# The first batch's last nine hidden units computed as sums of parts behind most of its down products

## Chip, cores and metric

The kernel runs on one core of a Trainium2 chip. The metric is device time in microseconds (us), the median of several runs. A page of one profiled execution and its trace go with it. The engines are TensorE (PE, with its weight loads as PEld), VectorE (DVE), ScalarE (ACT), GpSimd (POOL) and SyncE (SP), which issues nearly all the DMAs.

## The reference

Two blocks follow each other. The first is a linear attention on sketches: q and k of shape (4 batches, 4 heads, 1088 tokens, 32) are projected with S1 and S2 to 8 values each, and their outer product gives 64 features.

```python
def phi(x):
    a = np.einsum('rd,bhsd->bhsr', S1, x)
    b = np.einsum('rd,bhsd->bhsr', S2, x)
    return np.einsum('bhsi,bhsj->bhsij', a, b).reshape(*x.shape[:-1], r * r)
q_p, k_p = (phi(q), phi(k))
kv = np.einsum('bhsf,bhsd->bhfd', k_p, v)
z = np.sum(k_p, axis=2)
num = np.einsum('bhsf,bhfd->bhsd', q_p, kv)
den = np.einsum('bhsf,bhf->bhs', q_p, z)[..., None] + 1e-06
return (num / den).astype(np.float32)
```

The result, 4352 tokens of 128 values, is x of the second block, a SwiGLU feed-forward net with 1536 hidden values:

```python
g = x @ w_gate
silu = g * (1.0 / (1.0 + np.exp(-g)))
val = x @ w_val
return (silu * val @ w_out).astype(np.float32)
```

## The kernel before

Tokens lie along the free axis (`xT`, 128 x 4352). They are cut into blocks: 0, 1 and 2 are the first batch (384, 384 and 320 tokens), blocks 3 to 9 the other three batches (six of 480 and one of 384). The 1536 hidden values are 12 chunks of 128. A *unit* (i, j) is block i and chunk j: gate and value products into two PSUM banks, SiLU on ACT, the product of both on VectorE into a slot of `hbuf` or `late`. `down` (L1061) multiplies one such chunk with w_out and adds up 12 of them in one bank; `store` (L1120) transposes the sum on VectorE and writes it out.

A unit is computed in one of two ways. `unit` (L1026) uses two fp32 matmuls, each of which the profile shows as two records. `start_unit` (L990) and `finish_unit` (L1002) use parts: weights and tokens are cut into a high part, a scaled low part and a difference (`w1`, `wb`, `wd`; `x1`, `x0`, `xd`) of type fp32r, and the product is three fp32r matmuls of one record each. `start_unit` does the difference products (L997) and lets ACT scale both banks (L1000); `finish_unit` adds the other two products per bank (L1010, L1011), then ACT's SiLU (L1013) and VectorE's product (L1018). The parts of weights are made by `cut_weights` (L840), three chunks of 128 at a time ("chunk 3" of a weight below is its hidden chunks 9 to 11): ACT makes w1, VectorE (for wg) or POOL (for wv) the low part, ACT wb, and VectorE or POOL the difference. `cut_tokens` (L873) does the same for one block of tokens.

Before, blocks 0 to 2 are all computed with `unit`, and blocks 3 to 9 with the parts. The weights come as 64-bit numbers and are narrowed to fp32 by `narrow` (L245), with rotating buffers `exp` and `man`.

The attention of batches 1 to 3 runs beside this as a generator, `attentions` (L615): `parts_of(n)` lets it go n steps on. Its steps for a batch are transposes of k and q on VectorE, key products on TensorE (L354), key features on VectorE (L377), sums of the key features on POOL (`feature_sums`, L543), key values on TensorE (L388), query sketches (L342) with copies on ACT (L590), denominators and query features on VectorE (`query_step`, L741), and numerators on TensorE (L780).

Every engine works through its own list in the order in which the program writes it; semaphores keep the dependences. So the place of a step in this order decides what it stands behind on each engine. Around the change the order is written out by hand, in the loop over `seq` (L1300): 30 units of the first batch, from the 18th on (z = 17) with one down product and one step of the attention each, and with the pieces of `cut_weights` put between. Six early units keep SiLU and value apart (`late=True`), and `catch_up` (L1055) multiplies them later on POOL. After the loop the remaining down products run three at a time with further steps of the attention (L1345 to 1355), then the first main unit is started (L1358). The main loop (L1376) does 84 units.

PSUM has eight banks. `bank` hands out four single ones, `pair` the least recently used of three pairs that is not held, and `wide` the pairs named "a" and "b".

Of the kernel before, what the change touches and what calls it, by code (L numbers as in the profile page):

```python
# [19 lines left out]
def kernel(  # L20
# [223 lines left out]

    def narrow(dst, raw, shape, engine=nc.gpsimd, split=False):  # L245
# [14 lines left out]
            stage.tile(shape, I32, tag=n + tag, name=n, bufs=6) for n in ("exp", "man")  # L260
# [282 lines left out]
    def feature_sums(phk):  # L543

        rows = phk[:].rearrange("p c h i j -> p c (h i j)")
        s = apool.tile([P, 4, H * F], FP32, tag="zs", name="zs")
        add = lambda o, a, b: nc.gpsimd.tensor_tensor(out=o, in0=a, in1=b, op=ALU.add)

        def last():
            add(s[:, 0, :], s[:, 0, :], s[:, 1, :])  # L550
            add(s[:, 0, :], s[:, 0, :], rows[:, 8, :])

        return s[:, 0, :], [
            lambda: add(s[:, 0:2, :], rows[:, 0:2, :], rows[:, 4:6, :]),
            lambda: add(s[:, 2:4, :], rows[:, 2:4, :], rows[:, 6:8, :]),
            lambda: add(s[:, 0:2, :], s[:, 0:2, :], s[:, 2:4, :]),
            last,
        ]
# [56 lines left out]
    def attentions():  # L615
# [5 lines left out]
        hold("a")  # L621
        kp = wide("a")
# [11 lines left out]
        for n, (i, c0, c1) in enumerate(((0, 0, 3), (0, 3, 5), (1, 5, 7), (1, 7, 9))):  # L634
            first = H * (c0 - kpieces[i][0])
            kb = sketch(kp, i)[:, first : first + H * (c1 - c0), 1, :]
            key_features(phk, (ka[:, H * c0 : H * c1, :], kb), c0, c1)
            if n == 3:
                release("a")
            if n % 3 != 1:  # L640
                yield
        zs, sums = feature_sums(phk)
        for f in sums:
            f()
        yield from turn_keys(2)
        kvz = wide("a")
        key_values(kvz[:, 0, 0:F], phk, 0, NC)
        value_sums(kvz[:, 0, :], zs)
        kab, kcopies = sketched(wide("b"), key_products, 2, "kab2")
        fold(kvz[:, 0, :])  # L650
        spread = spread_out(1, kvz[:, 0, :])
        hold("a", "b")
        yield
        qab, copies = sketched(wide("a"), query_sketches, 3, "qab")
        run_copies(copies, 2)
        yield
        run_copies(kcopies, 2)
        release("a", "b")
# [165 lines left out]
    def homes(w):  # L824


        if w is wv:
            for c in range(4):
                yield [
                    stage.tile([P, 3, P], F32R, tag=tag, name=name, bufs=6)[:]  # L830
                    for tag, name in (("exp", "w1"), ("man", "wb"), (("exp", "man")[c % 2], "wd"))
                ]
        else:
            big = lambda pool, tag, bufs: pool.tile([P, 2, 3, P], F32R, tag=tag, name="g" + tag, bufs=bufs)
            for c in range(2):
                t = [big(stage, "raw", NRAW), big(stage, "raw", NRAW), big(apool, "phq", 2)]
                for k in range(2):
                    yield [x[:, k] for x in t]

    def cut_weights(w, lows, engine):  # L840
# [3 lines left out]
        for c, (w1, wb, wd) in enumerate(homes(w)):  # L844
            src = w[:, 3 * c : 3 * c + 3, :]
            low = lows[c]
            w_parts[id(w), c] = (w1, wb, wd)
            fine = dict(out=wd, in0=whole(w1), in1=whole(wb), **sub), engine.tensor_tensor
            if engine is nc.vector:
                fine = dict(  # L850
                    out=wd, in0=low, scalar=-BETA, in1=whole(w1), op0=ALU.mult, op1=ALU.add
                ), engine.scalar_tensor_tensor
            for row, f, args in zip(
                rows,
                (nc.scalar.activation, engine.tensor_tensor, nc.scalar.activation, fine[1]),
                (
                    dict(out=w1, in_=src, func=AF.Copy, scale=CUT),
                    dict(out=low, in0=src, in1=whole(w1), **sub),
                    dict(out=wb, in_=low, func=AF.Copy, scale=BETA),
                    fine[0],  # L860
                ),
            ):
                row.append((f, args))
# [9 lines left out]
    def cut_tokens(i, engine=nc.gpsimd):  # L873
# [21 lines left out]
        first, second = (difference, low) if engine is nc.vector else (low, difference)  # L895
# [94 lines left out]
    def start_unit(y):  # L990

        i, j = line[y // NCH], y % NCH
        n = blocks[i][1]
        xd = x_parts[i][2][:, 0:n]
        ps = sums_of[y] = pair(y)[:, :, 0:n]
# [6 lines left out]
    def finish_unit(y):  # L1002
        i, j = line[y // NCH], y % NCH
        n = blocks[i][1]
        x1, x0, _ = (x[:, 0:n] for x in x_parts[i])
        ps = sums_of.pop(y)
# [14 lines left out]
        let_go(y)  # L1021
# [39 lines left out]
    def down(y=None):  # L1061
# [3 lines left out]
        if j == 0:  # L1065
            acc[i] = bank("g1" if i == 1 else "g2" if i in line[2::2] else "acc")
# [231 lines left out]
    seq += [(i, j) for j0 in (6, 9) for i in range(3) for j in range(j0, j0 + 3)]  # L1298
    order = [(i, j) for i in range(3) for j in range(NCH)]
    for z, (i, j) in enumerate(seq):  # L1300
# [6 lines left out]
        if z in (24, 25, 26):  # L1307
            catch_up()
# [4 lines left out]
        if z >= 17:  # L1313
            todo.remove(order[0])
            todo.insert(0, order.pop(0))
            down()
        if z == 20:
            lows = [
                pool.tile([P, 3, P], FP32, tag=tag, name="low", bufs=bufs)[:]
                for pool, tag, bufs in ((apool, "qb", 2), (apool, "dT", 2), (apool, "rd", 2), (apool, "qb", 2))  # L1320
            ]
            first, low, second, third = cut_weights(wv, lows, nc.gpsimd)
        if z in (20, 21):
            take(first, 2)
        if z == 21:
            take(low, 3)
        if z == 25:
            take(second, 3)
        if z >= 17:
            parts_of(1)  # L1330
        if z == 26:
            take(low, 1)
            take(third, 3)
        if z == 29:
            take(second, 1)
            take(third, 1)
        if z == 23:
            lows = [room[:, 6 + c, :].rearrange("p (c f) -> p c f", f=P) for c in range(4)]
            gates = cut_weights(wg, lows, nc.vector)
        for row, at in enumerate(((23, 24), (25, 26, 27, 28), (27, 28))):  # L1340
            if z in at:
                take(gates[row], 4 // len(at))
    todo.sort()
    x_steps = None
    while len(todo) > 2:  # L1345
        for _ in range(min(3, len(todo) - 2)):
            down()
        if len(todo) < 9:
            take(gates[3], 2)
        if begun[0] and not x_steps:  # L1350
            x_steps = cut_tokens(HEAD, nc.vector)
            run(x_steps)
        parts_of(1 + (begun[0] and len(todo) > 2))
    while not begun[0]:
        parts_of(1)
    run(x_steps or cut_tokens(HEAD, nc.vector))
    hold("acc")
    start_unit(0)  # L1358
    while todo:
        down()  # L1360
# [15 lines left out]
    for y in range(END):  # L1376
        if y in GROUPS:
            group()
        if y in WIDE:
            finish_unit(y)  # L1380
        if y + 1 < END:
            start_unit(y + 1)
        if y not in WIDE:
            finish_unit(y)
# [52 lines left out]
```

## Time and profile before

| | |
|---|---|
| median of 3 runs | 278.81 us (278.68 to 279.05) |
| profiled execution | 278.89 us, its span 277.2 us |
| TensorE busy | 271.4 us, 98% of the span |
| VectorE busy | 203.7 us, 74% |
| ScalarE busy | 184.5 us, 67% |
| GpSimd busy | 98.9 us, 36% |
| down products (L1082) on the chain that ended last | 22% |
| fp32 units (L1034) on that chain | 16% |
| parts products (L997, L1010, L1011) on that chain | 13% each |
| first parts product of a main unit (L997) in the timeline | 91.42 us |

How to read it: a busy TensorE overlaps itself, since matmuls are pipelined; the pieces of the chain show how long each one holds the next. The idle time of an engine counts only where another one waits for it. A row of the timeline has the start, the duration, the engine, the line, and output and inputs by name.

### The profile page before, as it was taken

What the parts mean: (1) busy time and instruction counts of PE and PEld (TensorE: products, weight loads), DVE (VectorE), ACT (ScalarE), POOL (GpSimd) and SP (SyncE); (2) the same over time, 40 slices, a digit from 0 to 9 for tenths busy, and PEclk for the clock granted to TensorE, in tenths of its full rate; (3) what the DMA queues carried; (4) which work ended last, traced back from release to release, by engine and by line L of the source; (5) the groups of instructions that cost most, each with busy time, mean ns of one, the idle gap of its engine ahead of it and who ended that gap; (6) DMA issues with size and microseconds to landing.
All of it is one profiled execution on the core that took longest, in us unless ns stands there. A gap on an engine that the chain in (4) does not pass through costs nothing.

```text
span 277.2 us, 5670 instructions
## 1 busy us (share of the span) xinstructions
PE 271.4 (98%) x2169; PEld 198.3 (72%) x2169; DVE 203.7 (74%) x355; ACT 184.5 (67%) x330; POOL 98.9 (36%) x110
## 2 busy tenths in 40 slices
PE   8899999999999999999999999999999999999995
PEld 7645565666766787777577777867887888788994
DVE  3997987977688873887545766967877995987431
ACT  3468665565421586667479898769879878886860
POOL 3313422179820440060034353435425553542000
PEclk9999999999999999999999999999999999999999
DMA  6573195221151123000200020000100200010011
GB/s 192 168 220 79 54 277 185 74 89 57 39 114 28 26 85 94 2 1 0 38 13 4 0 39 0 0 2 10 27 0 2 36 0 1 9 29 0 10 29 28
DMA packets 26139, 14.30 MB, mean 52 GB/s; under 512 B 19840, under 2 KB 24192, under 8 KB 26112
## 3 DMA queue, kind: packets, MB, share of 16 engines
q1 hardware_dynamic: 25456, 13.84, 19.4%
q8 instruction: 17, 0.28, 0.4%
q10 hardware_dynamic: 656, 0.10, 0.2%
q14 instruction: 10, 0.08, 0.1%
HBM read 11.41 MB, written 2.23 MB: 49 GB/s over the span
## 4 chain that ended last, share of the span: by engine, by line
PE 94%; DVE 2%; DMA 2%; ACT 1%; issue 0%; SPq 0%
PE PS L1082 22%; PE PS L1034 16%; PE PS L1010 13%; PE PS L997 13%; PE PS L1011 13%; PE PS L1074 2%; PE PS L1077 2%; PE PS L1076 2%; PE PS L354 2%; PE PS L780 2%; PE PS L342 2%; PE PS L388 2%; DMA kld<-in_k_dram 2%; PE PS L1110 1%; PE PS L497 1%; PE PS L445 1%
## 5 line engine op out<-in xcount | busy, mean ns | idle before, releaser
L1000 ACT ACTIVATE PS<-PS 128x960 f32<-128x960 f32 (+1 forms) x84 | 78.5, 935 | 32.0 <-PE PS L997 31.2
L1018 DVE SCALAR_TENSOR_TENSOR hbuf<-PS,sg 128x480 f32<-128x480 f32 (+1 forms) x84 | 53.7, 640 | 43.6 <-ACT sg L1013 40.8
L1013 ACT ACTIVATE sg<-PS 128x480 f32<-128x480 f32 (+1 forms) x84 | 46.7, 556 | 2.0 <-PE PS L1011 1.2
L997 PE MATMUL PS<-xd,gphq 128*128 128x480 f32 (+1 forms) x84 | 47.3, 564 | 0.0
L1082 PE MATMUL PS<-hbuf,wo 128*128 128x480 f32 (+3 forms) x118 | 45.9, 492 | 0.0
L1010 PE MATMUL PS<-x,graw 128*128 128x480 f32 (+1 forms) x84 | 32.1, 382 | 0.0
L1011 PE MATMUL PS<-x,wb 128*128 128x480 f32 (+1 forms) x84 | 31.6, 376 | 0.0
L997 PE MATMUL PS<-xd,wd 128*128 128x480 f32 (+1 forms) x84 | 31.4, 374 | 0.0
L1010 PE MATMUL PS<-x,w 128*128 128x480 f32 (+1 forms) x84 | 31.4, 374 | 0.0
L1011 PE MATMUL PS<-x,graw 128*128 128x480 f32 (+1 forms) x84 | 31.3, 373 | 0.0
L1034 PE MATMUL PS<-xT,wg 128*128 128x384 f32 (+1 forms) x72 | 28.7, 480 | 0.0
L1034 PE MATMUL PS<-xT,wv 128*128 128x384 f32 (+1 forms) x72 | 28.0, 470 | 0.2 <-DVE wv L286 0.2
L1082 PEld LDWEIGHTS PS<-hbuf,wo 128*128 128x128 f32 x118 | 22.1, 189 | 7.4 <-issue 0.9
L1038 ACT ACTIVATE sg<-PS 128x384 f32<-128x384 f32 (+1 forms) x30 | 13.8, 465 | 18.8 <-PE PS L1034 17.2
L997 PEld LDWEIGHTS PS<-xd,gphq 128*128 128x128 f32 x84 | 15.8, 188 | 10.0 <-ACT PS L1000 6.4
L997 PEld LDWEIGHTS PS<-xd,wd 128*128 128x128 f32 x84 | 15.8, 189 | 9.9 <-issue 6.7
L884 POOL TENSOR_TENSOR x<-xT,x 128x480 fp32r<-128x480 f32 (+1 forms) x6 | 7.2, 1195 | 37.6 <-ACT x L881 37.6
L1034 PEld LDWEIGHTS PS<-xT,wv 128*128 128x128 f32 x72 | 13.4, 190 | 8.9 <-DVE hbuf L1049 0.9
L1034 PEld LDWEIGHTS PS<-xT,wg 128*128 128x128 f32 x72 | 12.9, 189 | 9.3 <-issue 1.2
L1010 PEld LDWEIGHTS PS<-x,graw 128*128 128x128 f32 x84 | 15.7, 187 | 3.5 <-ACT PS L1000 0.8
L1082 PE MATMUL PS<-hbuf,scaled 128*128 128x480 f32 x36 | 17.4, 565 | 0.0
L1010 PEld LDWEIGHTS PS<-x,w 128*128 128x128 f32 x84 | 15.8, 188 | 2.2
(184 smaller groups left out, 494.5 us busy)
## 6 DMA issues: line engine op xcount, KB each, us to landing
kld<-in_k_dram SPq DMA_DIRECT2D x4, 544.0 KB, 4.4
vld<-in_v_dram SPq DMA_DIRECT2D x12, 144.0 KB, 4.7
qld<-in_q_dram SPq DMA_DIRECT2D x3, 544.0 KB, 4.2
raw<-in_moe_w_out_dram SPq DMA_DIRECT2D x4, 384.0 KB, 4.0
raw<-in_moe_w_gate_dram SPq DMA_DIRECT2D x3, 384.0 KB, 3.6
raw<-in_moe_w_val_dram SPq DMA_DIRECT2D x3, 384.0 KB, 3.7
out_dram<-o SPq DMA_DIRECT2D x16, 60.0 KB, 2.0
vld<-in_v_dram SPq DMA_DIRECT2D x4, 112.0 KB, 4.3
```

The lines of the kernel that those rows point to most:

```text
L342: nc.tensor.matmul(ps[32 * a : 32 * a + 32, 96 * (c - c0) : 96 * (c - c0) + 96], qT[:, 4 * c + a, :], s123[:, a : a + H, :, :].rearrange(" ...
L354: nc.tensor.matmul(ps[32 * a : 32 * a + 64, 64 * (c - c0) : 64 * (c - c0) + 64], kT[:, c, a : a + 2, :].rearrange("p a t -> p (a t)"), s12 ...
L884: engine.tensor_tensor(out=x0[:, 0:n], in0=x, in1=whole(x1[:, 0:n]), op=ALU.subtract)
L997: nc.tensor.matmul(ps[:, k], w_parts[id(w), j // 3][2][:, j % 3, :], xd, start=True, stop=True)
L1000: nc.scalar.activation(ps, ps, AF.Copy, scale=-1.0 / WHOLE)
L1010: nc.tensor.matmul(ps[:, k], w1, x1, start=False, stop=False, skip_group_check=True)
L1011: nc.tensor.matmul(ps[:, k], wb, x0, start=False, stop=True, skip_group_check=True)
L1013: nc.scalar.activation(sg, ps[:, 0], AF.Silu, scale=WHOLE)
L1018: nc.vector.scalar_tensor_tensor(out=hj[:, 0:n], in0=ps[:, 1], scalar=WHOLE, in1=sg, op0=ALU.mult, op1=ALU.mult)
L1034: nc.tensor.matmul(o[:, 0:n], w[:, j, :], xT[:, t0 : t0 + n], start=True, stop=True)
L1038: nc.scalar.activation(sg[:, 0:n], g[:, 0:n], AF.Silu)
L1082: nc.tensor.matmul(acc[i][:, 0:n], w, hidden[i, j][:, 0:n], **sides)
```

## The change

The last nine units of the first batch, chunks 9 to 11 of blocks 0, 2 and 1, are no longer computed by `unit` but by `start_unit` and `finish_unit`, with parts of wg's and wv's chunk 3 and of the tokens of blocks 0, 2 and 1, which are made for it. The loop over `seq` ends after 27 units (its last four with one down each). Eight down products follow with steps of the attention, while chunk 3's parts and block 0's and 2's tokens are cut; then come the nine units with two downs each, while the other chunks' parts and block 1's tokens are cut; then the rest. The down products of the three blocks are interleaved, so three sums (banks g0, g1, g2) are open at the same time. `home` gives each chunk's parts a place (chunk 3 of wv has a new tile `v3`, of wg the room of "phq" buffers). The narrowing has 5 and 4 buffers instead of 6 and 6. The key sums are added in three steps of two rows, each put behind the features that it needs; key products and sketches take pairs that are free, instead of "a" and "b".

```diff
+    narrow_bufs = dict(exp=5, man=4)
...
-            stage.tile(shape, I32, tag=n + tag, name=n, bufs=6) for n in ("exp", "man")
+            stage.tile(shape, I32, tag=n + tag, name=n, bufs=narrow_bufs[n]) for n in ("exp", "man")
...
-            lambda: add(s[:, 0:2, :], rows[:, 0:2, :], rows[:, 4:6, :]),
-            lambda: add(s[:, 2:4, :], rows[:, 2:4, :], rows[:, 6:8, :]),
-            lambda: add(s[:, 0:2, :], s[:, 0:2, :], s[:, 2:4, :]),
+            lambda: add(s, rows[:, 0:2, :], rows[:, 2:4, :]),
+            lambda: add(s, s, rows[:, 4:6, :]),
+            lambda: add(s, s, rows[:, 6:8, :]),
...
-        hold("a")
-        kp = wide("a")
+        kp = pair("keys")
...
+            if n == 0:
+                zs, sums = feature_sums(phk)
+            else:
+                sums.pop(0)()
             if n == 3:
-                release("a")
+                let_go("keys")
...
-        kvz = wide("a")
-        key_values(kvz[:, 0, 0:F], phk, 0, NC)
-        value_sums(kvz[:, 0, :], zs)
-        kab, kcopies = sketched(wide("b"), key_products, 2, "kab2")
-        fold(kvz[:, 0, :])
+        kv = bank("g0")
+        key_values(kv[:, 0:F], phk, 0, NC)
+        kab, copies = sketched(pair(), key_products, 2, "kab2")
+        run_copies(copies, 2)
+        value_sums(kv, zs)
+        fold(kv)
...
+    def home(w, c):
+        if w is wg:
+            if c == 3:
+                return [big("phq", k) for k in range(3)]
+            return [big("raw", k) if k < 8 else big("phq", 3) for k in range(3 * c, 3 * c + 3)]
+        if c == 3:
+            t = const.tile([P, 3, 3, P], F32R, name="v3")
+            return [t[:, k] for k in range(3)]
...
-    def cut_weights(w, lows, engine):
+    def cut_weights(w, chunks, lows, engine):
...
-    def cut_tokens(i, engine=nc.gpsimd):
+    def cut_tokens(i, engine=nc.gpsimd, soon=False):
...
-        first, second = (difference, low) if engine is nc.vector else (low, difference)
+        first, second = (difference, low) if soon else (low, difference)
...
-    def start_unit(y):
-        i, j = line[y // NCH], y % NCH
+    def start_unit(i, j):
...
-            acc[i] = bank("g1" if i == 1 else "g2" if i in line[2::2] else "acc")
+            acc[i] = bank({1: "g1", 2: "g2"}.get(i, "g2" if i in line[2::2] else "acc"))
...
-    seq += [(i, j) for j0 in (6, 9) for i in range(3) for j in range(j0, j0 + 3)]
-    order = [(i, j) for i in range(3) for j in range(NCH)]
+    seq += [(i, j) for i in range(3) for j in range(6, 9)]
+    order = [(i, j) for j0, j1 in ((0, 6), (6, 9), (9, NCH)) for i in (0, 2, 1) for j in range(j0, j1)]
+    def next_down(n=1):
+        for _ in range(n):
+            todo.remove(order[0])
+            todo.insert(0, order.pop(0))
+            down()
...
         if z >= 17:
+            next_down()
             parts_of(1)
+        if z == 19:
+            gates3 = cut_weights(wg, (3,), [free_room(7)], nc.vector)
+            values3 = cut_weights(wv, (3,), [free_room(6)], nc.gpsimd)
+        if z >= 19:
+            take(gates3[z - 19], 1)
+            take(values3[z - 19], 1)
+    hold("g0", "g1")
+    for step in range(8):
+        if step != 3 and step < 6:
+            parts_of(1)
+        next_down()
+        for p in parts.get(21 + step, ()):
+            part(*p)
+        if step == 0:
+            take(gates3[2], 1)
+            take(values3[2], 1)
+            run(cut_tokens(0, nc.vector, soon=True))
+        if step == 1:
+            take(values3[3], 1)
+            take(gates3[3], 1)
+        if step == 4:
+            run(cut_tokens(2, soon=True))
+        if step == 5:
+            values = cut_weights(wv, range(3), [free_room(k) for k in range(3)], nc.gpsimd)
+        if step >= 5:
+            catch_up()
+            take(values[0], 1)
+    last = [(i, j) for i in (0, 2, 1) for j in range(9, NCH)]
+    start_unit(*last[0])
+    for u, at in enumerate(last):
+        if u in (1, 3):
+            finish_unit(*at)
+        if u + 1 < len(last):
+            start_unit(*last[u + 1])
+        if u not in (1, 3):
+            finish_unit(*at)
+        next_down(2)
+        if u != 1 and u < 7:
+            parts_of(1)
+        if u == 1:
+            gates = cut_weights(wg, range(3), [free_room(k) for k in (8, 9, 7)], nc.vector)
+        take(values[1 + u // 3], 1)
+        for row, first in enumerate((1, 2, 5)):
+            if first <= u < first + 3:
+                take(gates[row], 1)
+        if u == 3:
+            run(cut_tokens(1, soon=True))
+    take(gates[3], 3)
+    while not begun[0]:
+        parts_of(1)
+    next_down(2)
+    run(cut_tokens(HEAD, nc.vector, soon=True))
+    parts_of(2)
+    next_down(2)
+    parts_of(2)
+    hold("acc")
+    start_unit(HEAD, 0)
+    next_down(2)
+    release("g0", "g1")
```

## The prediction

> **What bounds the kernel now.** I read the page first, then the chain that ended last, then the busy time by stretches, then VectorE's timeline where the changed part begins. The page:
>
> ```profile
> span 277.2 us, 5670 instructions
> ...
> PE 271.4 (98%) x2169; PEld 198.3 (72%) x2169; DVE 203.7 (74%) x355; ACT 184.5 (67%) x330; POOL 98.9 (36%) x110
> ...
> PE   8899999999999999999999999999999999999995
> ...
> PE 94%; DVE 2%; DMA 2%; ACT 1%; issue 0%; SPq 0%
> ```
>
> TensorE is full from slice 3 on and carries 94% of the chain. So matmul time that is saved is time gained, but every stretch in which TensorE must wait is time lost. The profiled execution took 278.89 us for a span of 277.2, 0.08 over the median of 278.81; I add my sum to 278.89.
>
> The chain in order of time gives the true cost of a matmul (the busy means overlap each other):
>
> ```profile
> 49.17 0.65 PE PS L1082 x2
> 49.82 1.08 PE PS L1034 x4
> ...
> 56.92 1.20 PE PS L354 x36
> ...
> 60.25 1.29 PE PS L1034 x4
> ```
>
> An fp32 unit (four records) costs 1.29 us on a 384-column block (0 and 1) and 1.08 on the 320-column block 2; a down product 0.65 on 384 columns and half of 1.08, 0.54, on 320. The parts' matmuls of 384 columns, from the timeline late in the kernel:
>
> ```profile
> 248.20 0.34 PE L997 MATMUL PS<-xd,gphq 128*128 128x384 f32 x1
> 248.38 0.34 PE L997 MATMUL PS<-xd,wd 128*128 128x384 f32 x1
> 248.56 0.38 PE L1010 MATMUL PS<-x,graw 128*128 128x480 f32 x1
> 248.77 0.38 PE L1011 MATMUL PS<-x,graw 128*128 128x480 f32 x1
> ```
>
> Starts are 0.18 apart at 384 columns (0.175 is what 0.218 at 480 scales to), six of them to a unit. For 320 columns there is no row; 0.146 is scaled.
>
> Who has room beside TensorE? Busy time by stretches (columns: stretch, length, then PE, weight load, DVE, ACT, POOL, with the clock after them):
>
> ```profile
> 13.00:16.00 3.00, 2.56 (x54) 1.46 (x55) 2.84 (x12) 2.12 (x9) 0.45 (x1) 1.00 0.50 125
> 48.00:56.00 8.00, 8.00 (x28) 5.13 (x27) 7.63 (x17) 4.38 (x11) 1.05 (x2) 1.00 0.21 72
> 56.00:64.00 8.00, 8.00 (x58) 4.89 (x57) 6.16 (x11) 4.71 (x13) 6.54 (x7) 1.00 0.21 70
> 64.00:72.00 8.00, 8.00 (x135) 5.42 (x133) 5.98 (x11) 2.89 (x7) 7.76 (x9) 1.00 0.23 72
> 80.00:88.00 8.00, 8.00 (x87) 4.80 (x85) 7.58 (x10) 0.44 (x2) 1.76 (x1) 1.00 0.14 22
> ```
>
> VectorE (DVE) is 95% busy from 48 to 56, GpSimd (POOL) 97% from 64 to 72. They keep up there because TensorE still has thirteen fp32 units (about 16 us) to do beside them. That is the cover the change touches.
>
> **The gain.** Nine units move from fp32 to parts: six of 384 columns, 1.29 - 6 x 0.175 = 0.24 each, and three of 320, 1.08 - 6 x 0.146 = 0.20 each: 2.06 us of TensorE time. All other matmuls are the same in number and size. Fewer exp/man buffers only matter to the weight narrowing, where the same order stands and TensorE is not held by it: 0. The banks of the key products and sketches change; the products' own count and the DMAs (k, q, v loads, spread, stores) do not: 0, hidden beside the loss below.
>
> **The cost, place 1: the eight down products.** Up to unit (1,8), TensorE has the same list in both. Its down product starts at 49.17. From there the new order gives TensorE 4 downs (2.60), units (2,6) to (2,8) (3.24), key products (1.20), then (0,4), (0,5) (1.30) and (2,0) to (2,5) (3.24): it is out of work at 60.75 and needs chunk 3's wg and wv differences and block 0's token parts for the first `start_unit`.
>
> VectorE, in the same stretch of before:
>
> ```profile
> 54.45 0.49 DVE L1049 TENSOR_TENSOR late<-sg,PS 128x320 f32<-128x320 f32 x1
> 54.85 0.55 DVE L271 SCALAR_TENSOR_TENSOR exp<-raw,exp 128x384 int32<-128x384 int32 x1
> 55.32 0.55 DVE L277 SCALAR_TENSOR_TENSOR man<-raw,man 128x384 f32<-128x384 uint32 x1
> 55.79 0.70 DVE L578 STREAM_TRANSPOSE qT<-qld 128x512 f32<-128x512 f32 x1
> 56.49 0.56 DVE L1049 TENSOR_TENSOR hbuf<-sg,PS 128x384 f32<-128x384 f32 x1
> ```
>
> It is the same up to the query transpose and free at 56.41 (each starts 0.08 before the last ends). Then, in the new order: gate chunk 3's low part 0.87, first key features 0.95, to 58.1; it waits for block 0's high part, which ACT makes behind the value chunk's second activation, which waits for POOL's low part (ends 57.91): 57.91 + 0.51 + 0.51 = 58.95. Then xd and x0 of block 0 (0.55 each, like the 384-wide rows), two key features (0.68 each), two narrowing steps (0.55 each) and the gate difference (0.55): starts at 58.95, 59.42, 59.89, 60.49, 61.09, 61.56, 62.03, end 62.58. About 0.15 later TensorE starts: **2.0 lost**.
>
> Its second matmul needs the value difference, on POOL. POOL's order there: first key-sum add (from 60.65, when the second key features are there) 1.28, second 1.28, the wo narrowing 1.00, then the difference at 1.35 (mean of four, 0.99 to 1.76): 65.55. TensorE had come to 62.91: **2.8 lost**. `finish_unit` then waits for ACT to scale the two banks, 0.80 for 768 columns (scaled from 0.95 at 960): **0.8 lost**. After it stand downs (1,0) and (1,1), whose products are only made by `catch_up` on POOL, behind the third key-sum add 1.28, two of 0.74, block 2's x0 (0.9, scaled) and then 1.00 each: ready at 70.2 and 71.2, TensorE was there at 67.7: **2.65 and 0.3 lost**. Place 1: 8.55.
>
> **Place 2: the last nine units.** From 71.95 TensorE has 13.1 us of its own (attention matmuls 1.14 + 1.20 + 0.25 + 1.62, seven downs of 0.65 and one of 0.54, 3.8 of parts) and reaches 85.0, where `start_unit` needs block 1's xd. VectorE makes that behind the query denominators (sketches end 80.8, copies on ACT 1.0, SiLU and product 0.8, the five small steps 1.94 as from 76.65 to 78.59 now), a gate low part 0.87 and its own 0.55: 85.9. **1.05 lost**, and 0.3 more for the bank that the product behind it frees. The next bank comes free behind query features 0.95, their transpose 0.98, a gate low part 0.87 and the product 0.5: 89.55 against 88.25 for TensorE, **1.45 lost**.
>
> **Place 3: the handover to the main units.** xd of the first main block (0.65) waits on VectorE behind the numerators' copy (0.69) and three gate differences (0.55 each), about 0.5 longer than TensorE has downs for: **0.5 lost**. Behind it stand x0 0.65, four key features (0.95 and three of 0.69), a key transpose 0.84 and two output transposes (0.51, 0.56), less the overlaps 5.0; only the last of these frees the bank of the third unit started. TensorE's own work there is three halves of 0.44, two downs and four matmuls of 0.218, 3.3: **1.7 lost**. Places 2 and 3: 5.0.
>
> In before, TensorE is busy 8.00 of 8.00 in all these stretches, so nothing is given back. Sum: 278.89 - 2.06 + 8.55 + 5.0 = 290.4.
>
> **Between the bounds.** The rows above are mostly of an engine with its neighbour at rest. When VectorE and POOL work at once, the rows spread: a low part on VectorE 0.55 to 1.19, w - wb on POOL 0.99 to 1.76. In place 1 they both work without a pause, so I take two such meetings on the path, 1.5: **292**. Lower end: fastest rows everywhere, 1.1 less than 290.4 (the value difference 0.36, three gate low parts 0.3 each, rounded up), about 289. Upper end: the slowest rows for the four key-sum and difference steps (0.3 + 0.3 + 0.3 + 0.4) and the three low parts (0.3 each) on top of 292, about 294; with one more bank wait as long as place 2's 1.45, 296.
>
> [...]
>
> The emptiest row above (13 to 16 us) has TensorE busy 2.56 of 3.00 and the clock at 1.00, so no row here prices a longer idle time by the clock; I take 0 for it. [...]
>
> **The rivals.** *The cover holds* (the other side): VectorE and POOL finish chunk 3, the tokens and the catch-ups before TensorE asks; 278.89 - 2.06 = 276.8. For it: over the whole span they have 26% and 64% free. Against it: the 95% and 97% rows, in exactly this stretch. It decides once the three places together lose under 2.06 instead of 13.5, so VectorE's list from 56.41 to 62.58 would have to be done in a fraction of its rows. Chance 0.03. *Only place 1 loses*: VectorE's lists in places 2 and 3 get ahead while TensorE stands in place 1, since what is late there depends on margins of 1 to 2 us; 290.4 - 5.0 = 285.4. Against it: the denominators start from TensorE's own sketches, so they slip with it. Chance 0.13. *More than I take*: every meeting at its slowest and a further wait, the 296 above. For it: in before VectorE and POOL hardly ever run without a pause together (7.63 beside 1.05, 5.98 beside 7.76), in place 1 they do, so their slow rows may become the rule. Chance 0.19. *No change* within 0.2% (0.56 us, about what can be told from none): gain and loss cancel; 0.01. My forecast, 287 to 294 and most likely 292, has 0.64.
>
> The range 287 to 296 leaves out the first two rivals and the top of the third. Faster 0.03, same 0.01, slower 0.96.
>
> **What would show it.** Right: TensorE's row of slices loses its nines around 60 to 72 us, with matmuls of the first `start_unit` waiting for VectorE's and then POOL's weight-cut line, and a down product waiting for POOL's `catch_up` line; smaller gaps near 85 to 90 and 103 to 109; the start and everything after the second group of attention as before; nine units with six records at 0.18 or 0.15. Wrong: nines all through 60 to 72 (the cover holds); gaps in place 1 alone; or a clock below 1.00. My prediction fails most easily on the order of magnitude of the waits behind VectorE and POOL, since each waits on the other.

## The result, and the profile after

| | before | after |
|---|---|---|
| median of 4 runs | 278.75 us (278.66 to 279.05) | 295.38 us (295.17 to 296.88) |
| ratio | | 1.0606, 95% interval 1.0571 to 1.0642 |
| profiled execution | 278.89 us, span 277.2 | 296.88 us, span 295.2 |
| TensorE busy | 271.4 us | 276.6 us |
| TensorE's clock, mean of the profiled execution | 1.000 | 0.969 |

The change costs 16.6 us. The forecast was 292 and the range 287 to 296, so the time lies in the range, but above the forecast's own 287 to 294, where the rival "more than I take" stood with its 296. The executions of one kernel differ here in part by the share of time that TensorE ran at half clock: the four of after had mean clocks of 0.969, 0.977, 0.977 and 0.983.

The page of after. Compare the rows with those of before: TensorE's row has lost its nines in several slices from the ninth to the sixteenth (59 to 118 us, at 7.38 us a slice), and the row of clock digits has gaps there, where that of before has nines throughout.

```profile
span 295.2 us, 5728 instructions
...
PE 276.6 (94%) x2187; PEld 204.0 (69%) x2187; DVE 208.6 (71%) x359; ACT 192.6 (65%) x342; POOL 102.0 (35%) x112
...
PE   7899999937996988999999999999999999999995
...
PEclk9999999995897997999999999999999999999999
```

The waits of TensorE, longest first (engine and line, for what it waited, us in total, times, longest). The line numbers have moved: L1005 is `start_unit`, L1089 `down`, L880 `cut_weights`, L898 the tokens' difference, L1065 `catch_up`, L1131 the output transpose.

```profile
PE PS L1005 <- DVE gphq L880: 4.0, 1, 4.0
PE PS L1005 <- DVE xd L898: 2.8, 1, 2.8
PE PS L1005 <- DVE o L1131: 2.1, 1, 2.1
PE PS L1089 <- POOL hbuf L1065: 1.6, 1, 1.6
PE PS L1005 <- POOL v L880: 1.4, 1, 1.4
```

In before no wait of TensorE was over 0.9 us. All five belong to steps that the prediction had named: gate difference, block 1's `xd`, the output transpose that frees a bank, `catch_up`, value difference. (A sixth, 1.1 us for key transposes, lies in the load phase and cost nothing: these products start at 6.28 us, in before at 6.27.) The stretches (length, then PE, weight load, DVE, ACT, POOL, the clock after them):

```profile
56.00:64.00 8.00, 4.91 (x24) 3.01 (x18) 6.99 (x10) 3.39 (x9) 5.00 (x4) 1.00 0.21 73
64.00:72.00 8.00, 3.86 (x9) 2.58 (x10) 4.17 (x7) 1.99 (x3) 7.40 (x8) 0.58 0.21 70
72.00:80.00 8.00, 8.00 (x131) 5.48 (x131) 1.45 (x5) 2.42 (x5) 4.30 (x5) 0.78 0.02 4
80.00:88.00 8.00, 8.00 (x102) 6.20 (x101) 3.53 (x8) 5.64 (x13) 0.74 (x1) 1.00 0.33 83
88.00:96.00 8.00, 5.21 (x17) 3.85 (x16) 7.86 (x10) 3.20 (x7) 3.79 (x4) 0.79 0.00 0
...
104.00:112.00 8.00, 5.86 (x22) 3.73 (x21) 7.27 (x12) 3.19 (x6) 3.71 (x3) 1.00 0.25 39
112.00:120.00 8.00, 8.00 (x135) 6.57 (x134) 4.23 (x8) 5.59 (x9) 3.46 (x4) 0.79 0.37 96
```

Before had 8.00 of 8.00 and a clock of 1.00 in these stretches (56 to 120). Now four of them hold TensorE's gaps (two for place 1, one each for places 2 and 3 of the prediction), and four show a lower clock, each time in or just behind a gap. Taken over 65.3 to 75.5, 92.6 to 96.0 and 113.1 to 116.5 us alone, the clock is 0.50, and 1.00 outside: a mean of 0.58 over 8 us is 6.7 us at half, 0.78 is 3.5, and 0.79 is 3.4: 17.0 us together.

The half shows too in the pitch of equal matmuls in the timeline (start, duration). The starts of 480 columns are 0.22 apart up to 113 us and again after 116.48, and 0.40, nearly twice that, from 113.28 on:

```profile
112.55 0.38 PE L1018 MATMUL PS<-x,wb 128*128 128x480 f32 x1
112.76 0.38 PE L1005 MATMUL PS<-xd,graw 128*128 128x480 f32 x1
...
113.28 0.60 PE L1017 MATMUL PS<-x,graw 128*128 128x480 f32 x1
113.68 0.60 PE L1018 MATMUL PS<-x,graw 128*128 128x480 f32 x1
...
116.48 0.38 PE L1017 MATMUL PS<-x,w 128*128 128x480 f32 x1
116.70 0.38 PE L1018 MATMUL PS<-x,wb 128*128 128x480 f32 x1
```

Everything is lost by about 117 us: from there on the two kernels go through the main loop at the same pace (the last numerators start 18.1 us later than before, at 201.3 against 183.2; the profiled executions differ by 18.0).

### The profile page after: what moved, and what is told of

It is laid out like the page before. It is cut to its first block, busy times and chain, and to the rows that moved or that the text cites. A ratio compares the mean times of both kernels' runs of the same rounds, so it can differ in the third digit from the quotient of the medians.

```text
span 295.2 us, 5728 instructions
## 1 busy us (share of the span) xinstructions
PE 276.6 (94%) x2187; PEld 204.0 (69%) x2187; DVE 208.6 (71%) x359; ACT 192.6 (65%) x342; POOL 102.0 (35%) x112
## 4 chain that ended last, share of the span: by engine, by line
PE 84%; DVE 6%; POOL 3%; DMA 2%; ACT 2%; issue 1%; SPq 1%; DVEq 0%
PE PS L1089 18%; PE PS L1017 13%; PE PS L1005 13%; PE PS L1018 13%; PE PS L1041 10%; PE PS L1084 2%; PE PS L1081 2%; PE PS L1083 2%; PE PS L390 2%; PE PS L344 2%; DMA kld<-in_k_dram 1%; PE PS L356 1%; PE PS L781 1%; POOL zs L549 1%; DVE man L279 1%
## 5 line engine op out<-in xcount | busy, mean ns | idle before, releaser
L1008 ACT ACTIVATE PS<-PS 128x960 f32<-128x960 f32 (+2 forms) x93 | 85.3, 918 | 46.9 <-PE PS L1005 45.9
L1025 DVE SCALAR_TENSOR_TENSOR hbuf<-PS,sg 128x480 f32<-128x480 f32 (+2 forms) x93 | 58.5, 629 | 53.9 <-ACT sg L1020 48.4
L1020 ACT ACTIVATE sg<-PS 128x480 f32<-128x480 f32 (+2 forms) x93 | 50.9, 547 | 3.7 <-PE PS L1018 3.0
L1089 PE MATMUL PS<-hbuf,wo 128*128 128x480 f32 (+3 forms) x124 | 49.1, 503 | 1.6 <-POOL hbuf L1065 1.6
L1005 PE MATMUL PS<-xd,gphq 128*128 128x480 f32 (+2 forms) x51 | 29.5, 579 | 6.8 <-DVE gphq L880 4.0
L1089 PEld LDWEIGHTS PS<-hbuf,wo 128*128 128x128 f32 x124 | 23.4, 193 | 9.1 <-POOL hbuf L1065 2.6
L893 POOL TENSOR_TENSOR x<-xT,x 128x480 fp32r<-128x480 f32 (+2 forms) x8 | 9.0, 1128 | 51.6 <-ACT x L890 51.6
L1005 PE MATMUL PS<-xd,wd 128*128 128x480 f32 (+1 forms) x63 | 24.0, 380 | 2.1 <-DVE o L1131 2.1
L1017 PE MATMUL PS<-x,graw 128*128 128x480 f32 (+1 forms) x63 | 24.3, 386 | 0.0
L1018 PE MATMUL PS<-x,graw 128*128 128x480 f32 (+1 forms) x63 | 24.0, 380 | 0.0
L1017 PE MATMUL PS<-x,w 128*128 128x480 f32 (+1 forms) x63 | 23.7, 377 | 0.0
L1018 PE MATMUL PS<-x,wb 128*128 128x480 f32 (+1 forms) x63 | 23.7, 377 | 0.0
L1005 PE MATMUL PS<-xd,graw 128*128 128x480 f32 (+1 forms) x42 | 22.8, 543 | 0.1
L1041 PE MATMUL PS<-xT,wg 128*128 128x384 f32 (+1 forms) x54 | 21.4, 478 | 0.0
L1041 PE MATMUL PS<-xT,wv 128*128 128x384 f32 (+1 forms) x54 | 21.1, 471 | 0.2 <-DVE wv L288 0.2
L1005 PEld LDWEIGHTS PS<-xd,gphq 128*128 128x128 f32 x51 | 9.9, 194 | 13.7 <-issue 5.0
L1005 PEld LDWEIGHTS PS<-xd,wd 128*128 128x128 f32 x63 | 12.0, 191 | 10.0 <-issue 4.5
L1089 PE MATMUL PS<-hbuf,scaled 128*128 128x480 f32 x36 | 17.4, 564 | 0.0
L985 POOL TENSOR_TENSOR hlate<-hbuf,hlate 128x480 fp32r<-128x480 f32 x10 | 12.9, 1290 | 9.8 <-ACT hlate L984 7.7
L1041 PEld LDWEIGHTS PS<-xT,wg 128*128 128x128 f32 x54 | 9.7, 189 | 7.4 <-issue 1.2
L1041 PEld LDWEIGHTS PS<-xT,wv 128*128 128x128 f32 x54 | 10.0, 190 | 6.8 <-DVE hbuf L1056 0.9
```

The lines of the kernel that those rows point to most:

```text
L893: engine.tensor_tensor(out=x0[:, 0:n], in0=x, in1=whole(x1[:, 0:n]), op=ALU.subtract)
L985: add_to(before, y + 2, lambda: nc.gpsimd.tensor_tensor(out=h0, in0=h, in1=whole(h1), op=ALU.subtract))
L1005: nc.tensor.matmul(ps[:, k], w_parts[id(w), j // 3][2][:, j % 3, :], xd, start=True, stop=True)
L1008: nc.scalar.activation(ps, ps, AF.Copy, scale=-1.0 / WHOLE)
L1017: nc.tensor.matmul(ps[:, k], w1, x1, start=False, stop=False, skip_group_check=True)
L1018: nc.tensor.matmul(ps[:, k], wb, x0, start=False, stop=True, skip_group_check=True)
```

## The experiments

Two theories stood against each other. *Lists*: the three places are late because VectorE's and GpSimd's lists are too long for eight down products, and each wait is worth about its own length. *Clock*: the waits are dear because TensorE runs at half clock behind them, so filling them with anything gives much of the time back. A third question was whether the parts save anything at all. Every kernel below was timed against before; all differences "to after" are of medians (295.38), before being 278.75 to 278.87 each time.

**1. Keep TensorE busy in its waits.**

```diff
+            if k and fill:
+                keep_warm(fill, ps=bank("g0"))
...
+    keep_warm(15, ps=bank("g0"))
-    start_unit(*last[0])
+    start_unit(*last[0], fill=6)
...
+        if u == 5:
+            keep_warm(11, ps=bank("g0"))
...
+        if u == 0:
+            keep_warm(12, ps=bank("g0"))
```

> The changed kernel with TensorE's waits filled by 44 dummy bf16 matmuls of 512 columns into a bank that is free then (about 0.21 us each: 15 before the first unit's first matmul, 6 before its second, 12 before its down products, 11 before the seventh unit). They fit into the waits of 4.0, 1.4, 2.2 and 2.8 us that the changed kernel's trace shows, so no engine's list gets longer. Lists theory (TensorE waits for VectorE's and GpSimd's lists; the half clock comes on top): the granted clock stays at 1.00 until about 113 us, the matmuls behind the waits run at full rate, and the 3.9 us at 71.6 to 75.5 and 2.6 us at 92.6 to 96.0 of matmuls at half rate cost half as much: about 3.2 less than 295.4, 292. Clock theory (the half-rate stretches are most of the loss): most of the 16.6 goes, 284 or less. If the half rate lay hidden in waits: 295.

Measured: 293.98 (293.17 to 294.92), ratio 1.0544 (1.0514 to 1.0575), 1.4 less than after. Two of its four runs had a clock of 1.000 all through and took 293.17 and 293.30; so at full clock some 14.4 us of the 16.6 are still there (what the dummy matmuls themselves may hold up is in it). The clock row of its profiled execution has one gap left, behind the wait that was not filled:

```profile
PEclk9999999999999997999999999999999999999999
```

```profile
PE PS L1007 <- DVE o L1133: 2.0, 1, 2.0
```

The 15 dummy matmuls took the wait of 4.0 us down to 0.6, and the 11 that of 2.8 to 0.3, so one took about 0.23 us (3.4 / 15 and 2.5 / 11). The clock is 1.00 from 56 to 104 us, where after has its first two stretches at half. So the half clock follows from the waits, and it is worth about 2 us of a median execution; the lists are the larger part. The time is neither the 292 of the lists theory nor the 284 of the other, but nearer to the first.

**2. The last catch-ups earlier**, where GpSimd stands less behind the key sums.

```diff
+        if z in (11, 12, 13):
+            catch_up()
...
-            catch_up()
             take(values[0], 1)
```

> The changed kernel with the last three late products (catch_up on GpSimd) put at units 11 to 13 of the loop, where GpSimd is mostly idle, instead of behind the key sums. Lists theory: the two waits of a down product for GpSimd (1.65 and 0.45 in the trace) go, with what little stands before them, and nothing else in the first place changes: the waits for the gate difference (4.0) and the value difference (1.4) stay, places 2 and 3 stay. 2 to 3 less than 295.4: 292.5 to 293.5. Clock theory: TensorE still stands empty for 4 us, the half rate comes as before and the time stays within 1 of 295.4.

Measured: 294.29 (293.66 to 294.97), ratio 1.0562 (1.0542 to 1.0583). The wait of 1.6 us at `catch_up` is gone, the waits of 4.0, 2.8 and 2.1 stand unchanged, 1.1 for the value difference. The gain is 1.1, less than the wait. So the 292.5 to 293.5 of the lists theory was missed; the half clock came as before (mean clocks of 0.969 to 0.977), which only the other theory had said.

**3. As 2, with the nine units as fp32 matmuls in the new order** (the parts are still cut, nobody reads them).

```diff
-    start_unit(*last[0])
...
     for u, at in enumerate(last):
-        if u in (1, 3):
-            finish_unit(*at)
-        if u + 1 < len(last):
-            start_unit(*last[u + 1])
-        if u not in (1, 3):
-            finish_unit(*at)
+        plain_unit(*at)
         next_down(2)
```

> As e2, but the nine last units are computed with two fp32 matmuls each, in the changed kernel's order and banks; the parts of wg's and wv's chunk 3 and of the tokens of blocks 0, 2 and 1 are still made at their places (nobody reads the tokens' parts). Lists theory: the nine units wait for no parts, so TensorE has 9 fp32 units more of cover in its list (10.9 us) and the waits for the gate and value differences, the ACT scaling and block 1's parts go; it then waits for key features, key transposes and key sums behind the same lists, 3 to 4 us, and 2.5 in the handover, with 2.1 less gain: 5 to 7 over before, 284 to 286. If the parts' matmuls were not the point and the order of down products and attention was: as e2, 292 to 293. Clock theory: no wait is longer than 2.5, the clock stays at 1.00 and the time falls to about that of before, 279 to 281.

Measured: 289.62 (287.57 to 290.36), ratio 1.0375 (1.0332 to 1.0419). That is 4.7 less than 2, though TensorE has 2.06 us more to do. But it is 3.6 over the upper expectation: the order and the cuts, with nobody waiting for a part in the first batch, still cost over 10 us. Its waits are others: 2.0 us for the output transpose, 1.3 for the key sums, 1.1 for key features and 1.1, in two pieces, for key transposes. Each of its executions also has some half clock (means of 0.988 to 0.994), which is in the 10 us.

**4. Two of the three long key-sum additions left out**, the first of them moved behind the last key features. Rows 4 to 7 are then missing from batch 1's key sums, and its denominators are of fewer keys.

```diff
-            else:
-                sums.pop(0)()
             if n == 3:
+                sums[0]()
+                del sums[:3]
                 let_go("keys")
```

> The changed kernel without the second and third of the three two-row adds of batch 1's key sums on GpSimd, and with the first put behind the last key features; it leaves rows 4 to 7 out of batch 1's key sums, so its denominators of batch 1 are of fewer keys. Contention theory (VectorE's operations with two SBUF inputs are held while GpSimd works, 1.24 and 1.61 us instead of 0.55 for the two narrowing steps beside the key sums): these two fall to about 0.55, the gate difference ends 1.7 earlier, the wait for it falls from 4.0 to about 2.3, and the time by about 1.5 to 2, to 293.5. If the long steps had another cause: they stay long, the wait for the gate difference stays at 4.0, and the time falls by under 0.5, for the late products behind the value difference only.

Measured: 294.29 (293.59 to 296.54), ratio 1.0568 (1.0525 to 1.0612). VectorE's narrowing steps in after, with the key sums on GpSimd (L549) at the same time (start, duration):

```profile
61.15 1.26 POOL L549 TENSOR_TENSOR zs<-phk 128x512 f32<-128x512 f32 x1 [2.71 <-DVE phk L379]
61.59 1.24 DVE L273 SCALAR_TENSOR_TENSOR exp<-raw,exp 128x384 int32<-128x384 int32 x1
62.49 1.46 POOL L549 TENSOR_TENSOR zs<-zs,phk 128x512 f32<-128x512 f32 x1
62.75 1.61 DVE L279 SCALAR_TENSOR_TENSOR man<-raw,man 128x384 f32<-128x384 uint32 x1
```

and without these sums (this execution runs 1.5 us later here, which the last section takes up):

```profile
63.08 0.55 DVE L273 SCALAR_TENSOR_TENSOR exp<-raw,exp 128x384 int32<-128x384 int32 x1
63.55 0.55 DVE L279 SCALAR_TENSOR_TENSOR man<-raw,man 128x384 f32<-128x384 uint32 x1
```

```profile
PE PS L1005 <- DVE gphq L880: 2.2, 1, 2.2
```

The same two instructions take 1.24 and 1.61 us beside the sums and 0.55 each without them, and the wait for the gate difference falls from 4.0 to 2.2. So it is shown that VectorE's steps are long because GpSimd adds at the same time. In after the two sums end at 62.41 and 63.95, and VectorE's two steps 0.42 and 0.41 us behind them, at 62.83 and 64.36. In the total, 1.1 us came back of the 1.8 of the wait, less than the 1.5 to 2 expected; the four executions lie 3 us apart.

**5. Block 1's tokens cut one unit earlier.**

```diff
-        if u == 3:
+        if u == 2:
             run(cut_tokens(1, soon=True))
```

> The changed kernel with block 1's token parts cut one unit earlier (after the third of the nine units instead of the fourth), so that they stand on VectorE ahead of the query denominators. Lists theory: the wait of 2.8 for block 1's xd goes; part of it comes back as waits of 0.5 to 0.7 for banks, since the denominators and features behind it are that much later: 1 to 1.5 less than 295.4, 294 to 294.4. If the wait was really for the sketches behind which the denominators stand: no change, 295.

Measured: 295.29 (293.78 to 296.90), ratio 1.0578 (1.0519 to 1.0637): no difference to after that could be told, where 294 to 294.4 was expected. The wait of 2.8 us for `xd` is gone, and another takes its place:

```profile
PE PS L1005 <- DVE hbuf L1025: 1.9, 1, 1.9
```

Its product on VectorE stands behind the query denominators and a gate low part (1.35 us):

```profile
89.84 0.48 DVE L1025 SCALAR_TENSOR_TENSOR hbuf<-PS,sg 128x320 f32<-128x320 f32 x1
```

This is the first bank of the prediction's place 2, its 0.3, which after had hidden behind the longer wait. It is longer here because TensorE comes to it earlier, while VectorE's list before that product is the same but for `xd`.

**6. Chunk 3's parts and block 0's tokens cut at z = 12 to 16**, under the fp32 units, instead of 19 and behind the loop. (The changed loop has 21 units, z = 0 to 20; six more fp32 units stand ahead of it, which makes the 27.)

```diff
-        if z == 19:
+        if z == 12:
             gates3 = cut_weights(wg, (3,), [free_room(7)], nc.vector)
...
+        if z == 16:
+            run(cut_tokens(0, nc.vector, soon=True))
```

> The changed kernel with wg's and wv's chunk 3 and block 0's tokens cut beside units 12 to 16 of the loop instead of from unit 19 on. Lists theory: the waits for the gate difference (4.0) and the value difference (1.4) go or fall under 0.5, but TensorE then meets the late products of GpSimd that stand behind the key sums, and waits 4 to 5 there instead of 2; about 3 less than 295.4, with the half clock as before, 292 to 293. If only chunk 3's place were the fault: all of place 1's 8 goes, 286 to 287.

Measured: 294.64 (294.30 to 295.13), ratio 1.0555 (1.0523 to 1.0587), 0.7 less than after, not the 3 expected. The waits of 4.0 and 1.4 are gone, and the wait for `catch_up` is 4.0 instead of 1.6, as expected; two new ones of 1.1 and 1.2 us, for a `late` product and for key features, came with it. What TensorE waited for first had hidden what it waited for next.

**7. Edits 2, 5 and 6 together**, and **8. the same without the last two steps of the attention before the first main unit** (they come in the main loop).

```diff
     parts_of(2)
     next_down(2)
-    parts_of(2)
     hold("acc")
```

> Late products early (as e2), block 1's tokens earlier (as e5) and chunk 3 and block 0's tokens earlier (as e6), together. Lists theory: no wait over 1 is left before the handover, so no half clock in place 1; what stays are 0.4 to 0.8 for banks behind VectorE in the nine units (2.5 together), 1 in the loop where VectorE now has more to do, and 2.5 in the handover: about 5 over before at full clock, 284 to 286. If the three waits were not one list's but independent: 295.4 less the single gains (2.1, 1.2, 3), 289 to 290.

> As e7, and without the last two steps of the attention before the first main unit (they follow in the main loop, which takes one step a unit), so that the last output transpose and the main units' products stand ahead of the key transposes on VectorE. Lists theory: the handover's wait of 2.0 to 2.5 falls under 0.5 and with it the half clock behind it: 2 to 4 less than e7, 281 to 283. If the handover's wait was for the output DMAs that hold the transpose's buffers: as e7.

Measured: 289.90 (287.25 to 290.92), ratio 1.037 (1.0309 to 1.043), and 285.56 (285.47 to 285.71), ratio 1.0228 (1.0193 to 1.0262), with a clock of 1.00 in all four executions of 8. The three edits that alone brought 1.1, 0.1 and 0.7 bring 5.5 together, and the fourth 4.3 more. Part of the 4.3 goes with the clock: the one execution of 7 at a clock of 1.000 took 287.25, 1.7 over 8, and the other three, with some half clock (means of 0.988 to 0.994), 289.42 to 290.92. Both times are above what the lists theory expected (284 to 286, and 281 to 283); 7 has the time of its rival (289 to 290), but not from the single gains that the rival added up (2.1, 1.2 and 3). The waits of 8 that are over 1 us, but for one of 1.1 in the load phase, at 6.4 us:

```profile
PE PS L1041 <- DVE late L1056: 2.6, 2, 1.5
PE PS L1005 <- DVE hbuf L1025: 2.4, 2, 1.9
PE PS L1005 <- DVE phk L379: 1.2, 1, 1.2
```

All three are VectorE's: the parts cut under the early fp32 units now make those late (L1041 is `unit`), and the nine units still wait for banks. The program holds g0 and g1 for the open sums from the eight down products on, and one of the three pairs lies on these banks, so the nine units take turns on two.

**9. As 8, with the nine units as fp32 matmuls**, and **10. as 9, without the three cuts of the first batch's tokens**, which nobody reads then.

> The order of the work is that of e8_all_np; alone the last nine units of the first batch are fp32 matmuls again, as in the kernel before, in the place and order that the change gave them. The parts of chunk 3 and of the tokens are still cut and are read by nobody in those units. Theory (the parts cost the bank of sums more than they save): six fp32 units of 384 columns and three of 320 put about 2.1 us of work back on TensorE, but each gives VectorE and ScalarE longer for the features before, so that the waits of 2.4 us for the product of features and of 1.2 us for the key features go: 282 to 285, under the 285.56 of e8_all_np. Rival (the parts are a net gain, the rest of the loss is the order): the 2.1 us come on top, 287 or more.

> As e9_fp32np, and the three cuts of the first batch's tokens are left out too, since nothing reads them once the nine units are fp32. What is left of the change is its order: eight down products after the third unit, then nine units with three sums open. Theory: the cuts take about 1.5 us of VectorE and as much of POOL in a stretch where VectorE is 0.8 to 1.0 busy, so 0.3 to 1 us less than e9_fp32np. Rival (only the order costs): same as e9_fp32np within 0.5 us, and both stay 3 us or more over the kernel before.

Measured: 282.88 (282.69 to 283.09), ratio 1.0138 (1.0104 to 1.0171), and 281.20 (280.89 to 281.44), ratio 1.0079 (1.005 to 1.0108). The stretch from 64 to 72 and the one from 80 to 88 in 8:

```profile
64.00:72.00 8.00, 6.82 (x135) 5.30 (x135) 5.86 (x9) 2.92 (x6) 7.35 (x8) 1.00 0.24 69
...
80.00:88.00 8.00, 5.58 (x27) 4.10 (x26) 7.76 (x13) 4.52 (x10) 3.99 (x4) 1.00 0.07 17
```

and in 9:

```profile
64.00:72.00 8.00, 8.00 (x133) 5.35 (x132) 7.15 (x11) 2.19 (x5) 7.35 (x8) 1.00 0.22 71
...
80.00:88.00 8.00, 8.00 (x28) 5.06 (x28) 7.72 (x14) 3.90 (x9) 3.52 (x3) 1.00 0.00 0
```

With fp32 units TensorE has no gap there, though VectorE is no less busy (7.15 against 5.86 us, and 7.72 against 7.76). So in the best order that was tried, reading the parts in the nine units costs 285.56 - 282.88 = 2.7 us net, where their shorter matmuls save 2.06: what their waits bring with them is worth 4.7, and 3.6 of it are the gaps in these two rows. Cutting the tokens for it costs another 1.7. The theory of 9 held (282 to 285). In 10 the gain is larger than the 0.3 to 1 expected.

**11. After, with only the edit of 8.**

> The changed kernel without the last two steps of the attention before the first main unit (they come later, in the main loop); places 1 and 2 are untouched. Theory (place 3 costs its wait of 2.06 us and the half clock of 3.4 us that follows it, 1.7): the first goes and the second with it, 291 to 292, and no stretch at half clock after 100 us. Rival (the wait is only a share of the lists' lag and comes back in the main loop, or the half clock belongs to the earlier waits): 293 to 295.

Measured: 293.50 (293.39 to 293.89), ratio 1.0527 (1.051 to 1.0545), 1.9 less than after. The wait of 2.1 us is gone (no wait for an output transpose is left), and so is the half clock behind it in the profiled execution (480 columns start 0.21 to 0.24 apart from 110.00 to 112.42). So the wait was not for the output DMAs that hold the transpose's buffers, the other cause named in the expectation of 8. The median gained about the wait alone; it misses the theory's 291 to 292 and is one of the rival's times (293 to 295), though the wait did not come back. The third stretch at half clock may be one of the profiled execution of after alone: it was the slowest of the four by 1.5 us, and 3.4 us at half clock cost 1.7.

No version was faster than before. Version 10 is nearest, 2.4 us behind; what these 2.4 are made of was only followed in part: TensorE is busy for 7.52 and 7.42 of 8 us from 40 to 48 and 48 to 56, where before has 8.00 twice, which is 1.1, with a wait of 1.1 us for a `late` product.

## Why the prediction was right, point by point

The prediction gave points in time for TensorE. Beside those of the profiled execution (a ready time of the prediction is taken with its 0.15 until TensorE starts):

| TensorE | predicted | after | late by |
|---|---|---|---|
| out of work, place 1 | 60.75 | 60.92 | 0.2 |
| first gate difference product | 62.73 | 64.89 | 2.2 |
| first value difference product | 65.7 | 66.70 | 1.0 |
| down (1,0), behind `catch_up` | 70.35 | 71.57 | 1.2 |
| out of work, place 2 | 85.0 | 88.46 | 3.5 |
| block 1's first difference product | 86.05 | 91.25 | 5.2 |
| first main unit | 101.2 | 106.01 | 4.8 |

(101.2 is 91.42 of before - 2.06 + 8.55 + 1.05 + 0.3 + 1.45 + 0.5. 60.92 and 88.46 are the starts less the idle times of 3.97 and 2.79 before them.)

**The gain, 2.06**: right in size. The parts' matmuls start 0.17 to 0.18 apart at 384 columns and 0.14 to 0.15 at 320, as scaled.

**Place 1, 8.55**: right within 1 us. From 60.92 to 71.57 are 10.65 us, which hold eight part products of 0.175, 1.4: 9.25 lost, where the prediction has 8.25 up to there (the last 0.3 of its 8.55 comes behind it). The four waits are 4.0, 1.4, 0.2 and 1.65 against 2.0, 2.8, 0.8 and 2.95; they follow each other, so what the first takes the next need not. The first is the term that was mis-sized: the two narrowing steps at 0.55 took 1.24 and 1.61, which is 1.75 of the 2.2 that the first product came late (experiment 4). The chain that ended last goes as the prediction had it, through GpSimd's third key sum, the two short ones, block 2's x0 and the catch-up:

```profile
66.65 1.50 POOL zs L549
...
68.21 0.74 POOL zs L549
...
69.02 0.73 POOL zs L549
69.75 0.82 POOL x L893
70.56 0.96 POOL hbuf L1065
...
71.57 2.93 PE PS L1089 x4
```

The last row also shows two downs (four records) in 2.93 us, where two took 2 x 0.65 = 1.30 in before: they run at half clock, which makes 2.6.

**The clock, taken at 0**: the step that failed. "No row here prices a longer idle time by the clock" was true of before, and 0 was the wrong choice out of it; a clock below 1.00 was also one of its own signs of being wrong. Half clock on TensorE's path cost 2.0 us from 71.57 to 75.5, which is most of the 2.3 added between the down and place 2 (1.2 to 3.5 late), 1.7 from 92.6 to 96.0, and 1.7 from 113.1 to 116.5 in the profiled execution: 5.4 of the 6.5 us by which that execution, 296.88, is over the sum of 290.4 without contention. The other terms nearly cancel: the down product came 1.0 and place 2 another 1.7 later, mostly by contention, and the bank waits of place 2 and the first wait of place 3 (2.25) did not show. Part of the 5.4 would have been waited for otherwise: experiment 1 gives about 2 for a median execution. The three stretches at a clock of 0.50 lasted 10.2 us (65.3 to 75.5), 3.4 and 3.4, and began behind waits of 4.0, 2.8 and 2.1 us.

**Contention, 1.5**: right in kind, and shown by experiment 4, but it hit place 2 as well. There VectorE's last small step of the denominators, the gate low part and `xd` took 1.21, 1.35 and 1.34 us with GpSimd cutting block 1's x0 and value differences at the same time:

```profile
87.37 1.21 DVE L753 TENSOR_TENSOR qab<-qab,den 128x288 f32<-128x288 f32 x1
88.50 1.35 DVE L880 TENSOR_TENSOR room<-wg,graw 128x384 f32<-128x384 f32 x1
89.77 1.34 DVE L898 SCALAR_TENSOR_TENSOR xd<-x,xT 128x384 fp32r<-128x384 f32 x1
```

In experiment 5, one unit earlier, `xd` took 0.56 and L753 0.46. So the 1.05 of place 2 became 2.8.

**Place 2's banks, 0.3 and 1.45**: did not show as waits, because the wait for `xd` was longer and let the banks come free behind it. Experiments 5 and 8 brought the first out, at 1.9, and experiments 1 and 8 the second, the one behind the query features, at 0.5.

**Place 3, 0.5 and 1.7**: the first was not seen, the second was 2.06, at the step that was named (the output transpose, 110.97 to 111.51 on VectorE, behind the key features and the key transpose). The prediction's terms for TensorE's own work there make 3.5, as in the trace (106.01 to 109.50), and not its 3.3, so by them 1.5 is lost.

**The rivals.** *The cover holds* fell with the first wait. *Only place 1 loses* fell with the waits of 2.8 and 2.1 us behind it. *More than I take* has the right time, for a reason that is half its own: the slow rows did become the rule in place 1, but more of the excess is the clock, which was not in it.

**The range**: that 295.38 still lies under 296 is partly luck. The 296 was added up from slow rows and one more bank wait, and the half clock took that room. The lower end has no working either: the fastest rows give about 289 (their terms make 1.26, not 1.1), and no term leads on to 287.

**"Nothing is given back"** held: no matmul of the main loop came earlier again.

## What to carry to other kernels

Shorter matmuls are a gain only while something else covers the other engines. Here a change that saved TensorE 2.06 us took away nine of the thirteen long units under which VectorE and GpSimd had worked, and even in the best order the saved work cost 2.7 us net: ask of a faster unit what its longer form had been hiding.

Waits in a row hide each other. Taking out one of several gave 0.1 to 1.9 us, three together 5.5 (the executions of one version lie up to 3.7 us apart, so the single gains are rough); so a wait's length in the profile is neither what its removal brings nor a bound on it, and a ledger is best kept in points in time.

If a forecast opens a gap in a TensorE that had none, price the clock too, from both sides, even though no row of before can show it: here 17.0 us at a clock of 0.50 lay in or just behind the gaps of one execution.

## What was not expected of the hardware

Half clock followed not only the gap in place 1 but single waits of 2.8 and 2.1 us with TensorE busy on both sides, and then lasted 3.4 us each time (a clock of 0.50 from 92.6 to 96.0 and from 113.1 to 116.5) though TensorE worked without a pause (busy 3.40 of 3.40 in both). It did not follow them in every execution (mean clocks of 0.969 to 0.983 for one kernel).

Two kernels whose edits are all later (experiments 4 and 6) show such a stretch once in their profiled executions between 4 and 12 us (a mean clock of 0.79 there in both), where before and after have 1.00; in experiment 4 that execution was the slowest of four, 296.54 against 293.59 to 294.59. In both, TensorE waited 1.5 and 1.6 us for key transposes, in the other profiled executions at most 1.2 at a time. Whether that is what brought it stays open.
